# DeltaNet and MLP-mixer on one core: keys copied on chip, a copy moved behind two others, transposes moved among products, and a new order of issue

## The chip, the cores and the metric

The kernel runs on one core of a Trainium2 chip. The metric is the device time of one execution in microseconds (us). A run on one core has no sibling cores to compare with, so a run counts as slow when it is over 1.5% above the fastest run of the same kernel on the same chip, and verdicts use the other runs. The engines are TensorE (PE; its weight loads are PEld), VectorE (DVE), ScalarE (ACT), GpSimd (POOL) and the issuing engine for DMA (SP). PEclk is the share of TensorE's full clock that its throttle granted.

## The reference

```python
# B=4 batches, H=8 heads, S=768 steps, D=48; q, k, v, beta are inputs, all fp32
k_n = k / (norm(k) + 1e-6)
for t in range(S):
    y[:, :, t] = q_t @ state
    state += beta_t * outer(k_t, v_t - state^T k_t)
x = y as (B, S, H*D)                       # 4 x 768 x 384
u = x + (relu(x^T @ w_tok1) @ w_tok2)^T     # token mixer
out = u + relu(u @ w_ch1) @ w_ch2           # channel mixer
```

## The kernel before

The recurrence is done in chunks of 64 steps: 48 steps of it, 12 for each batch. Each chunk needs the inverse of a triangular matrix (groups of chunks share one inversion on VectorE, a long chain of small subtractions and additions), then a few matmuls p_q, p_w, p_s. The mixers of a batch follow when its 12 steps are done. The whole kernel is written as generators, called jobs; each `yield` ends a piece of work, and a long string says which job does its next piece. Every engine executes its own pieces in the order in which that string issued them.

One step of the recurrence (cut):

```python
            p_q = ps_seq([128, NP, 2 * D], "p_q")
            for p in range(NP):
                nc.tensor.matmul(p_q[:, p], kqt[:, 2 * p + cc], s0[:, p])
            yield
            for i in range(2):                       # VectorE, two subtractions
                nc.vector.tensor_tensor(out=r_bd[...], in0=p_q[lo, ...], in1=v_st[...], op=ALU.subtract)
            nc.scalar.copy(y, p_q[hi])               # ScalarE, the copy of y
        ...
        yield
        p_w = ps_seq([128, NP, 2 * D], "p_w")        # TensorE, needs r_bd
        ...
        yield
        for r, e in zip(PAR, ends):
            nc.scalar.copy(w_bd[r, :, e], p_w[lo, :, e])   # ScalarE, the copies of w
        yield
        p_s = ...                                    # TensorE, needs w_bd
```

In the built program the copy of y waits for the two subtractions that were issued just ahead of it.

The channel mixer (cut), and the matmuls that only keep TensorE's clock up:

```python
        for c in range(0, NCH, 2):
            u_t = ...                                # transposes p_ut of two chunks of u, copied to u_t by ScalarE
            for m in range(NM):
                p_c = ...                            # u_t times wc1; ReLU of p_c on ScalarE
            ...                                      # eight products p_o with wc2, each added to xb by VectorE

    def keep_warm(m):                                # job x: m=1 (128 columns), job z: m=4 (512 columns)
        while True:
            nc.tensor.matmul(p_warm[:, 0:m], zero, zero[:, None, :].to_broadcast([128, m, 128]))
            yield
```

## Time and profile before

| before | value |
|---|---|
| runs (us) | 750.45, 755.32, 749.22 |
| profiled run (us) | 748.09 |
| first p_c matmul, start of the dense stage (us) | 166.7 |
| last matmul (us) | 742.4 |
| TensorE gaps over 0.15 us between them, sum (us) | 23.9 |
| of these, the largest three (us) | 11.31, 3.16, 2.75 |

Up to the first p_c, VectorE and the chain through it set the pace ("the start" below). From there TensorE does ("the dense stage"), and what counts is whether it ever stands still. The lines are shown in the prediction.

### The profile page before, as it was taken

Reading aid. Unit: us, or ns where it says so; the run is one execution under the profiler, and the core shown is the slowest. Engines: PE = TensorE matmul, PEld = TensorE weight load, DVE = VectorE, ACT = ScalarE, POOL = GpSimd, SP = SyncE. Lnnn points to the kernel's source line nnn. Section 1 sums busy time; section 2 is a strip of 40 time slices with the busy share of each in tenths; the row PEclk is TensorE's granted clock in tenths of the full one; section 3 lists DMA queues with packets and bytes.
Section 4 is the critical chain, followed back from the end, with each engine's and each line's share of the span. In section 5 each row is a group of like instructions: output and inputs, shape, how many; then the busy total and the mean of one; then the engine's idle time right before and its main releaser. Section 6 shows DMA issues by size and latency. Waiting matters only on the chain. (4 is left out here: it accounts for less than half of the span.)

```text
span 746.3 us, 18528 instructions
## 1 busy us (share of the span) xinstructions
PE 700.5 (94%) x7734; PEld 598.1 (80%) x7734; DVE 438.7 (59%) x1163; ACT 237.1 (32%) x553; POOL 100.7 (13%) x118
## 2 busy tenths in 40 slices
PE   8889998899999999999899998999949999999997
PEld 5558876568789899868888987879939987998987
DVE  6987688998878934349744688334753332321312
ACT  4546375535522123323144321133112322011120
POOL 1222135214330101020111110010000000000000
PEclk9997599999999999999999999999969999999999
DMA  8843356645544033251134210211010100000000
GB/s 164 170 101 78 83 123 144 163 107 121 106 89 89 1 87 61 42 116 33 38 71 88 50 43 29 57 32 33 22 27 11 40 7 1 13 10 22 0 22 22
DMA packets 151107, 46.92 MB, mean 63 GB/s; under 512 B 142416, under 2 KB 145488, under 8 KB 151024
## 3 DMA queue, kind: packets, MB, share of 16 engines
q1 hardware_dynamic: 151024, 45.74, 28.4%
q8 instruction: 61, 1.00, 0.6%
q14 instruction: 22, 0.18, 0.1%
HBM read 36.27 MB, written 9.44 MB: 61 GB/s over the span
## 5 line engine op out<-in xcount | busy, mean ns | idle before, releaser
L813 PE MATMUL p_c<-u_t,wc 128*128 128x256 f32 x864 | 198.8, 385 | 12.7 <-ACT u_t L782 12.7
L813 PEld LDWEIGHTS p_c<-u_t,wc 128*128 128x128 f32 x864 | 162.2, 192 | 34.6 <-ACT u_t L782 13.5
L833 PE MATMUL p_o<-wc,r 128*128 128x192 f32 x720 | 127.6, 328 | 3.5 <-ACT r L820 3.5
L833 PEld LDWEIGHTS p_o<-wc,r 128*128 128x128 f32 x720 | 116.6, 190 | 5.7 <-ACT r L820 4.3
L820 ACT ACTIVATE r<-p_c 128x512 f32<-128x512 f32 x72 | 42.6, 597 | 126.8 <-PE p_c L813 117.7
L786 DVE TENSOR_TENSOR xb<-xb,p_o 128x192 f32<-128x192 f32 x84 | 29.4, 351 | 75.9 <-PE p_o L833 75.5
L525 DVE TENSOR_TENSOR x<-x,sub 128x84 f32<-128x84 f32 (+24 forms) x178 | 60.9, 342 | 6.1
L520 DVE TENSOR_TENSOR sub<-x 128x84 f32<-128x84 f32 (+24 forms) x178 | 58.1, 326 | 4.2
L806 DVE TENSOR_TENSOR s<-r 128x384 f32<-128x384 f32 x24 | 14.0, 583 | 76.9 <-ACT r L820 76.9
L833 PE MATMUL p_o<-wc,s 128*128 128x192 f32 x288 | 52.8, 333 | 3.1 <-DVE xb L786 3.1
L233 POOL TENSOR_TENSOR w_f<-w_f,d 128x384 uint32<-128x384 uint32 (+1 forms) x34 | 34.4, 1015 | 125.2 <-DVE w_f L226 65.7
L833 PEld LDWEIGHTS p_o<-wc,s 128*128 128x128 f32 x288 | 47.4, 193 | 4.1 <-DVE xb L786 3.6
L323 POOL TENSOR_TENSOR v_st<-v_st,nrm 128x384 f32<-128x384 f32 x24 | 21.2, 884 | 209.1 <-DMA v_st<-in_v_dram 137.6
L704 ACT COPY xb<-p_q 64x384 f32<-64x384 f32 x33 | 15.7, 475 | 101.5 <-DVE rw_bd L700 101.4
L382 POOL TENSOR_TENSOR mb<-mask_c,cs 128x512 f32<-128x512 f32 x20 | 22.5, 1125 | 163.3 <-DVE cs L364 157.6
L408 DVE TENSOR_TENSOR gm<-p_g,mb 128x512 f32<-128x512 f32 x48 | 31.8, 685 | 14.6 <-PE p_g L402 13.9
L729 DVE TENSOR_TENSOR s_bd<-s_bd,p_s 48x192 f32<-48x192 f32 x60 | 21.4, 357 | 32.1 <-PE p_s L721 31.2
L782 ACT COPY u_t<-p_ut 128x384 f32<-128x384 f32 x24 | 10.6, 481 | 81.7 <-PE p_ut L778 81.6
L696 PEld LDWEIGHTS p_q<-s_bd,kqt 128*128 128x128 f32 x264 | 33.0, 191 | 3.7 <-issue 1.9
L700 DVE TENSOR_TENSOR rw_bd<-p_q,v_st 64x192 f32<-64x192 f32 x66 | 23.1, 349 | 21.6 <-PE p_q L696 11.1
L166 PE MATMUL p_warm<-warm 128*128 128x128 f32 (+1 forms) x102 | 35.5, 458 | 0.0
L696 PE MATMUL p_q<-s_bd,kqt 128*128 128x96 f32 x264 | 35.0, 275 | 0.3 <-DVE s_bd L729 0.2
(110 smaller groups left out, 1002.4 us busy)
## 6 DMA issues: line engine op xcount, KB each, us to landing
d<-in_moe_w_ch_dram SPq DMA_DIRECT2D x24, 384.0 KB, 3.8
kpad<-in_k_dram SPq DMA_DIRECT2D x24, 192.0 KB, 4.1
kst<-in_k_dram SPq DMA_DIRECT2D x96, 48.0 KB, 3.1
qpad<-in_q_dram SPq DMA_DIRECT2D x24, 192.0 KB, 3.4
v_st<-in_v_dram SPq DMA_DIRECT2D x96, 48.0 KB, 2.7
out_dram<-xb SPq DMA_DIRECT2D x24, 192.0 KB, 1.9
n_dram<-gm SPq DMA_DIRECT2D x72, 32.0 KB, 1.9
gm<-w_dram SPq DMA_DIRECT2D x72, 32.0 KB, 2.2
```

The lines of the kernel that those rows point to most:

```text
L166: nc.tensor.matmul(p_warm[:, 0:m], zero, zero[:, None, :].to_broadcast([128, m, 128]))
L233: nc.gpsimd.tensor_tensor(out=f, in0=f, in1=lo, op=ALU.add)
L382: scaler.tensor_tensor(out=mb, in0=mask_c[:, None, None, :].to_broadcast([128, NP, 2, C]), in1=cs[:, :, :, None].to_broadcast([128, NP, 2, ...
L408: nc.vector.tensor_tensor(out=blocks(gm)[:, :, cc, 0 : 2 * C].rearrange("s p (two n) -> s p two n", two=2), in0=p_g[cc], in1=mb[:, :, cc, ...
L520: nc.vector.tensor_tensor(out=tmp, in0=y[:, :, 0:s, s : s + 1].to_broadcast([n, k, s, w]), in1=y[:, :, s : s + 1, s + 1 : m].to_broadcast( ...
L525: nc.vector.tensor_tensor(out=y[:, :, 0:s, s + 1 : m], in0=y[:, :, 0:s, s + 1 : m], in1=tmp, op=ALU.add,)
L696: nc.tensor.matmul(p_q[:, p], kqt[:, 2 * p + cc], s0[:, p])
L700: nc.vector.tensor_tensor(out=r_bd[r, :, ends[i ^ cc]], in0=p_q[lo, :, ends[i]], in1=v_st[r, :, cc], op=ALU.subtract,)
L786: nc.vector.tensor_tensor(out=xb[:, c, e], in0=xb[:, c, e], in1=p, op=ALU.add)
L813: nc.tensor.matmul(p_c[:, k], piece_of(wc1, cb, f * 128)[:, f * 128 : (f + 1) * 128], u_t[:, cb], start=(cb == 0), stop=(cb == NCB - 1),)
L820: nc.scalar.activation(r2[:, m], p_c, ACTF.Relu)
L833: nc.tensor.matmul(p, a[:, m], wc2[:, m, j], start=(start and m == 0), stop=(m == NM - 1), skip_group_check=True,)
```

## The change

The intent: fewer small DMA transfers in the first 40 us, a copy of y that no longer makes ScalarE wait for VectorE, transposes of u that no longer stand in a row before p_c, and an order of issue made for all that. The diff, with the order string cut:

```diff
-            if src is k:
+            if src is k and u >= RU:
                 yield from stacked(kst, k, u)
+
+        heads = kpad[u % NK].rearrange("t (p par) d -> t p par d", par=2)
+        for cc in range(2 if u < RU else 0):
+            for par in range(2):
+                nc.scalar.copy(kst[PAR[par ^ cc], :, cc], heads[PAR[cc], :, par, 0:D])
+                yield
@@ recurrence
-            nc.scalar.copy(y, p_q[hi])
@@
             nc.scalar.copy(w_bd[r, :, e], p_w[lo, :, e])
+        if c > 0:
+            nc.scalar.copy(y, p_q[hi])
         yield
@@ mixer
-        for c in range(0, NCH, 2):
+        def turn_pair(c):
             u_t = mlp_pool.tile([128, NCB, 2 * U], FP32, name="u_t", bufs=1)
             for i in range(2):
                 turn(u_t, c + i)
                 yield
+            return u_t
+
+        u_t = yield from turn_pair(0)
+        for c in range(0, NCH, 2):
@@ after the first product
             add(c, 0, p_o)
             yield
+            if c + 2 < NCH:
+                u_t = yield from turn_pair(c + 2)
@@ order
-    w1*3 y w1 w3 y b w3*3 k0*4 y k0 w1 k0 x y z y*2 w3 z p0 b y b y k1 p0 k1 p0*2 y p0*8
     ... (60 lines)
+    b y w3*3 w1 k0 y k0 x k0*2 k3 k0*2 p0*2 y p0 y b*2 p0*3 k1*2 p0 w3 p0*3 k1*2 k2 k1 x
     ... (60 lines)
```

## The prediction

> **What bounds the kernel now.** I read the page first, then the busy time of each engine in stretches of 20 us, then TensorE's own timeline for its gaps, then the timeline of all engines around the largest gaps.
>
> ```profile
> PE 700.5 (94%) x7734; PEld 598.1 (80%) x7734; DVE 438.7 (59%) x1163; ACT 237.1 (32%) x553; POOL 100.7 (13%) x118
> PE   8889998899999999999899998999949999999997
> DVE  6987688998878934349744688334753332321312
> PEclk9997599999999999999999999999969999999999
> ```
>
> Two stages have different limits. Up to about 165 us, TensorE's row is high partly because of the matmuls that only keep it warm (51 wide and 216 small ones in the program), and DVE's row is at 7 to 9: the first VectorE addition of the token mixer (L772) starts at 160.7 us with 142.4 us of VectorE work ahead of it (the durations of the 354 instructions before it, added up). Single gaps over 0.15 us on VectorE come to 21 us there, 6.5 of them before 13.2 us and 10.3 between 67 and 102 us, where it waits for the first recurrence steps. So VectorE sets the pace of the first stage. From the first p_c matmul (166.7 us) to the last (742.4 us) TensorE sets it. I added up its remaining instructions at their warm spacing (p_c 0.216 us a pass, p_o 0.163, and so on): 553.7 us of the 575.7. The rest is gaps.
>
> The timeline of TensorE around 540 us shows the largest gap (start, us, engine, line, operation, in brackets the idle time before it and what ended it):
>
> ```profile
> 539.50 0.60 PE L586 MATMUL p_z<-t,gm 32*32 32x32 f32 x27
> 551.42 18.23 PE L813 MATMUL p_c<-u_t,wc 128*128 128x256 f32 x72 [11.31 <-ACT u_t L782]
> ```
>
> The same stretch for all engines, with lines left out:
>
> ```profile
> 549.57 0.72 DVE L700 TENSOR_TENSOR rw_bd<-p_q,v_st 64x192 f32<-64x192 f32 x2
> ...
> 550.38 0.48 ACT L704 COPY xb<-p_q 64x384 f32<-64x384 f32 x1 [11.94 <-DVE rw_bd L700]
> ...
> 550.88 0.48 ACT L782 COPY u_t<-p_ut 128x384 f32<-128x384 f32 x1
> ```
>
> TensorE waits for the second copy of u_t. That copy is ready from 539 us, but it stands on ScalarE behind the copy of y (L704), which waits for the two L700 subtractions, which stand on VectorE behind some 11 us of the inversion (L520, L525). At 457 us the same copy of y holds up three ReLU evictions:
>
> ```profile
> 457.90 0.48 ACT L704 COPY xb<-p_q 64x384 f32<-64x384 f32 x1 [9.15 <-DVE rw_bd L700]
> ...
> 458.40 1.57 ACT L820 ACTIVATE r<-p_c 128x512 f32<-128x512 f32 x3
> ...
> 459.06 4.17 PE L833 MATMUL p_o<-wc,r 128*128 128x192 f32 x24 [3.16 <-ACT r L820]
> ```
>
> All TensorE gaps over 0.15 us after the first p_c: 11.31, 3.16, 2.75 (363 us, an addition of p_o that is late on VectorE), 0.68 twice (p_c waits for u_t at 682 and 713 us), 0.65 (a transpose of u, 438 us), and eleven smaller ones that sum to 4.7; together 23.9 us.
>
> **What the Trainium skill says.** "PSUM — Partial Sum Buffer", section "Engine vs sequencer instructions": "ScalarE/VectorE/GpSimdE queues are strict FIFO." The trace agrees: the copy of u_t starts 0.50 us after the copy of y that it doesn't depend on. "TensorE: Matmul & The Clock Gate", Part 1: after about 3.4 us without work the array falls back to half its clock until it has been busy again. The trace agrees: 0.66 granted in 540 to 560 us, and 72 passes of p_c took 18.23 us after the gap against 15.81 in the last pair, 2.4 us more. "DMA: Bandwidth & Descriptors", "Specifications": pieces under 512 B don't reach line rate. A row of kst is 48 floats, 192 B; 142416 of 151107 packets are under 512 B, and the DMA engines are 79 to 86% busy at 159 to 184 GB/s in the first 40 us. "SBUF — State Buffer", "Who interferes with whom": a VectorE operation with two inputs in SBUF contends with GpSimd's reads. The trace agrees: an L525 addition of 128x168 took 1.06 us beside GpSimd at 361 us and 0.33 us alone at 457 us.
>
> **The change, part by part.**
>
> *First keys on chip.* For four units 4 DMAs of 48 KB each become 4 ScalarE copies of 64x192. Removed: 16 issues, which fill about 0.65 us each of the issuing queue (2.58 to 3.16 us for each set of four), 10.9 us of a queue that runs without a break until 41 us. Added: 16 copies by some 0.31 us (the row L716, same shape), 5.0 us on ScalarE, which has 17.5 us of work in the first 33 us. The first unit gains nothing: its kpad, issued at about 2.1 us as now, lands some 4 us later (the median of the row kpad), four copies and the square take 1.8 us, so VectorE gets its first sum at about 8 us, as now (7.95). And from 13.2 us to the first inversion (33.4 us) VectorE has one gap over 0.15 us, 0.28 us; in the built program 71 VectorE instructions stand ahead of that inversion before and after, 27.5 us each. A relief of DMA can't shorten that. Gain: 0 to 1 us.
>
> *Copy of y behind those of w.* In the program the copy of y then needs no wait of its own: it comes after w, so the subtractions are long done. What stood behind it on ScalarE no longer waits for VectorE's inversion. This removes most of the 3.16 us; I take 2.5. The cost: p_s takes the PSUM buffer of p_q (two buffers in rotation p_q, p_w, p_s), so it now has to wait for the copy of y, 0.45 us later than for w. In the program TensorE has under 1.25 us of other work between p_w and p_s in 9 of the 33 steps with this copy; there p_s started 0.17 us after w so far, so each loses some 0.3 us: plus 2.5 us.
>
> *Transposes of u among the products.* 8 of 12 pairs get them after the first product instead of after the last. The 0.68 twice and some of the 0.65 go: minus 1.5 us. The second PSUM buffer comes free in time, since three transposes (0.65 us) cover the first copy (0.48 us).
>
> *New order.* In the order of before, 10.6 us of VectorE and no TensorE work stand between the last p_z and the p_c of the 11.31 us gap; in the new one no stretch of the program after the first p_c has more than 1.5 us of VectorE or ScalarE work without a matmul. The last inversion's chain, with what stands between, is 36.3 us of VectorE beside 43.1 us of TensorE work, where it was 30.3 beside 26.9. So the gap goes, and its half clock: minus 11.3 and minus 2.4. The other late chains are as uneven as before (33.1 beside 31.2, 25.0 beside 23.7, 30.8 beside 30.1 us), so I keep the 2.75 and the small gaps. TensorE work after the first p_c is 551.9 us against 553.7: minus 1.8. Ahead of the first L772 VectorE has 141.9 us against 142.4; it could lose some of its 10 us of waiting in the first steps, or gain some: minus 0.5. Eight fewer wide warm matmuls lie where TensorE isn't the bound: 0.
>
> The sum: -0.5 (keys) -2.5 + 2.5 (y) -1.5 (u) -11.3 -2.4 -1.8 -0.5 (order) = -18.0 us. 750.45 - 18.0 = 732.4 us.
>
> **Rivals.** (1) The inversion stays the limit and the wait only moves: p_w stands on TensorE's own queue and needs the same subtractions, so a late VectorE stops TensorE itself rather than ScalarE. For it: VectorE is still heavier than TensorE in three of the chains; 2.75 us of such waiting is there now. Against: the last chain, where the loss was, now has the larger TensorE side. It would give back 5 to 8 us: 738 to 741. (2) The copy of y on the path of p_s costs in all 33 steps rather than 9, up to 0.45 us each: plus 12 us more at the worst, 744. Against: in most steps p_s started 0.2 to 5 us after w, behind other matmuls. (3) The start is bound by DMA after all, through data that VectorE gets early enough only by chance, and the freed 10.9 us of the queue bring the whole first stage forward by 5 us or more: 727 or less. Against: VectorE's gapless 20 us. (4) The freed queue only makes later loads collide, and ScalarE (22.5 us of work ahead of the first inversion, 17.5 before) delays unit after unit: plus 2 to 3 us.
>
> **Range and chances.** The 13.7 us of the one gap are the safest part; the other terms are small and of both signs, and an order of some thousand steps can hide a new wait of a few us anywhere. I put eight in ten on 723 to 743. The border of 2% is at 735.4, 3 us above my number: faster 0.62, same 0.36, slower 0.02.
>
> **What would show it.** Right: no TensorE gap over 4 us after the first p_c, granted clock of 1.00 there throughout, gaps summing to 8 to 13 us; the first p_c between 162 and 168 us; copies of y with no wait for L700 in front of them; p_s waiting for ScalarE by up to 0.45 us in some steps; the first inversion still near 33 us with VectorE gapless before it. Wrong: a new gap of several us at a p_w that waits for L700, or the first p_c earlier than 160 or later than 171 us.

## The result, and the profile after

The changed kernel took 731.05 us (median of 733.07, 731.02, 731.08 and 730.3), the kernel before 749.86 us beside it. The ratio is 0.9738, with a 95% interval of 0.9688 to 0.9788: faster. A ratio here and below is the mean time of one kernel's fast runs over that of the other's of the same rounds, so it isn't quite the ratio of the medians that are quoted.

The number is within 1.4 us of the prediction, which is luck in part: the profile shows that two errors in it cancelled. Of the profiled runs (748.09 and 733.07 us, 15.0 apart where the medians are 18.8 apart):

| us | before | after | measured change | predicted |
|---|---|---|---|---|
| first p_c | 166.7 | 174.6 | +7.9 | -1.0 (keys -0.5, order -0.5) |
| first p_c to last matmul | 575.7 | 553.0 | -22.7 | -17.0 (all other terms) |
| gaps in that stretch | 23.9 | 6.3 | -17.6 | -12.8 (-11.3, -2.5, -1.5, +2.5) |

The page of the kernel after, busy time and the rows of slices:

```profile
PE 700.8 (96%) x7774; PEld 605.5 (83%) x7774; DVE 439.8 (60%) x1163; ACT 242.1 (33%) x569; POOL 99.4 (14%) x118
...
PE   8797998999999999999999999999999999999998
DVE  5998678799796792545965559723776432311212
...
PEclk9987579899899999999999999999999999999999
```

The hole in TensorE's row at 540 us is gone, and the clock is full from the twelfth slice on. But PEclk has its lowest digits, 7 and 5, in the fourth to sixth slice (55 to 110 us), at a place that the prediction left out of its sum. The kernel before has a 7 and a 5 there too.

What TensorE waited for between 176 us and the end, in the kernel after (waiter, releaser, us in total, times, longest):

```profile
PE p_o L844 <- DVE xb L793: 3.0, 4, 0.9
PE p_z L592 <- DVE t L587: 0.9, 2, 0.6
PE p_q L702 <- DVE s_bd L741: 0.7, 1, 0.7
PE p_q L702 <- DVE s_bd L736: 0.6, 1, 0.6
PE p_o L844 <- ACT u_t L789: 0.6, 2, 0.3
PE p_w L718 <- DVE rw_bd L706: 0.5, 1, 0.5
```

This is the whole answer: nothing over 0.9 us. p_c waits for nothing, and p_s is not in the list, though the prediction charged it 2.5 us.

The timeline that matters most is not where the old gap was. It is around 346 us in the kernel after (start, us, engine, line, operation, lines left out):

```profile
345.55 1.10 PE L702 MATMUL p_q<-s_bd,kqt 128*128 128x96 f32 x8 [0.61 <-DVE s_bd L736]
...
348.35 15.71 PE L824 MATMUL p_c<-u_t,wc 128*128 128x256 f32 x72
...
351.15 0.60 ACT L831 ACTIVATE r<-p_c 128x512 f32<-128x512 f32 x1 [1.82 <-PE p_c L824]
...
365.07 0.72 DVE L706 TENSOR_TENSOR rw_bd<-p_q,v_st 64x192 f32<-64x192 f32 x2
...
365.85 0.88 PE L718 MATMUL p_w<-rw_bd,gm 128*65 128x96 f32 x8
```

The two subtractions (L706) end over 19 us after their p_q, because the inversion stands ahead of them on VectorE. In the kernel before, the worst was 17.5 us and the one of the 11.31 us gap 11.6 us. So the new order doesn't bring the subtractions earlier; here it brings them later than ever. What is different is that 72 passes of p_c and six ReLUs run meanwhile, because the copy of y is not there to block ScalarE. None of the 33 copies of y has a wait over 0.15 us in front of it; in the kernel before 27 of them waited for L700. That put the prediction's attribution in doubt: it gave the 11.3 us to the order and 2.5 us to the move of y.

### The profile page after: what moved, and what is told of

Read it like the earlier page. It is cut to its first block, busy times and chain, and to the rows that moved or that the text cites.

```text
span 730.9 us, 18603 instructions
## 1 busy us (share of the span) xinstructions
PE 700.8 (96%) x7774; PEld 605.5 (83%) x7774; DVE 439.8 (60%) x1163; ACT 242.1 (33%) x569; POOL 99.4 (14%) x118
## 3 DMA queue, kind: packets, MB, share of 16 engines
q1 hardware_dynamic: 146672, 44.95, 28.7%
## 4 chain that ended last, share of the span: by engine, by line
PE 67%; DVE 22%; ACT 3%; issue 3%; DMA 2%; SPq 1%; POOL 0%; ACTq 0%; DVEq 0%; POOLq 0%
PE p_o L844 20%; PE p_c L824 16%; DVE sub L526 6%; DVE x L531 5%; PE p L762 4%; PE p_q L702 4%; PE p_s L728 3%; PE p_w L718 3%; PE p_g L408 3%; PE p_h L775 3%; PE p_z L592 2%; PE p_x L601 2%; PE p_warm L166 1%; PE p_warm L176 1%; DVE gm L414 1%
## 5 line engine op out<-in xcount | busy, mean ns | idle before, releaser
L824 PE MATMUL p_c<-u_t,wc 128*128 128x256 f32 x864 | 195.6, 381 | 0.0
L721 ACT COPY rw_bd<-p_w 64x192 f32<-64x192 f32 x72 | 22.4, 311 | 99.1 <-PE p_w L718 98.1
L844 PE MATMUL p_o<-wc,s 128*128 128x192 f32 x288 | 51.0, 329 | 2.5 <-DVE xb L793 2.5
L408 PE MATMUL p_g<-kqt 64*64 64x128 f32 x768 | 30.8, 304 | 7.3 <-ACT kqt L397 7.3
L736 DVE TENSOR_TENSOR s_bd<-s_bd,p_s 48x192 f32<-48x192 f32 x60 | 21.4, 357 | 25.9 <-PE p_s L728 25.0
L706 DVE TENSOR_TENSOR rw_bd<-p_q,v_st 64x192 f32<-64x192 f32 x66 | 23.0, 349 | 20.2 <-PE p_q L702 14.1
L728 PEld LDWEIGHTS p_s<-rw_bd,gm 128*112 128x112 f32 x288 | 32.9, 178 | 2.7 <-issue 0.3
```

The lines of the kernel that those rows point to most:

```text
L408: nc.tensor.matmul(p_g[cc][PAR[i ^ cc], p], kqt[PAR[i], 2 * p + cc, 0], kqt[PAR[i], 2 * p + cc],)
L728: nc.tensor.matmul(p_s[0 : C + D, p], gm[:, 2 * p + cc, C:], w_bd[:, p])
L824: nc.tensor.matmul(p_c[:, k], piece_of(wc1, cb, f * 128)[:, f * 128 : (f + 1) * 128], u_t[:, cb], start=(cb == 0), stop=(cb == NCB - 1),)
L844: nc.tensor.matmul(p, a[:, m], wc2[:, m, j], start=(start and m == 0), stop=(m == NM - 1), skip_group_check=True,)
```

## The experiments

Twelve kernels were run. They combine the three edits of code (K: keys on chip, Y: copy of y behind w, U: transposes of u among the products) with the order of before, that of after, or a splice: the order of before up to the first step of the token mixer, then the order of after with the pieces already done left out. Each splice and each single edit issues the same work; only the warm matmuls differ in number. "First p_c", "dense" and "gaps" are from the profiled run of each kernel, worked out as in the table above; "clock" is PEclk at 80 to 100 us.

| kernel | edits, order | first p_c | dense | gaps | clock | median (before beside it) | ratio (95%) |
|---|---|---|---|---|---|---|---|
| before | none, before | 166.7 | 575.7 | 23.9 | 0.61 | 749.86 | 1 |
| after | K Y U, after | 174.6 | 553.0 | 6.3 | 0.50 | 731.05 (749.86) | 0.9738 (0.969 to 0.979) |
| y_alone | Y, before | 163.7 | 556.9 | 8.9 | 1.00 | 727.42 (749.14) | 0.9756 (0.967 to 0.984) |
| order_alone | none, after | slow run | slow run | | | 767.40 (749.14) | 1.0208 (1.007 to 1.035) |
| undo_y | K U, after | 172.7 | 569.6 | 18.7 | 0.53 | 748.30 (749.14) | 1.0025 (0.999 to 1.006) |
| undo_keys | Y U, after | 175.7 | 550.9 | 6.2 | 0.54 | 732.27 (749.14) | 0.9806 (0.972 to 0.989) |
| parts_old_order | K Y U, before | 159.0 | 560.3 | 10.5 | 1.00 | 729.54 (748.61) | 0.9738 (0.969 to 0.978) |
| start_old | Y U, splice | 168.8 | 549.6 | 5.2 | 0.83 | 724.18 (748.61) | 0.9685 (0.964 to 0.973) |
| start_old_keys | K Y U, splice | 172.6 | 552.9 | 6.2 | 0.62 | 722.76 (748.61) | 0.9683 (0.963 to 0.974) |
| undo_u | K Y, after | 176.2 | 561.8 | 14.7 | 0.50 | 743.14 (748.61) | 0.9961 (0.993 to 0.999) |
| warm_new | K Y U, after, +16 warm | 176.0 | 552.3 | 6.5 | 1.00 | 732.67 (748.86) | 0.9818 (0.977 to 0.987) |
| warm_old | Y U, splice, +16 warm | 177.4 | 552.1 | 5.5 | 1.00 | 734.55 (748.86) | 0.9848 (0.980 to 0.989) |
| light_new | K Y U, after, +6 warm | 165.3 | 550.6 | 4.8 | 1.00 | 724.04 (751.96) | 0.9659 (0.961 to 0.970) |
| light_old | K Y U, splice, +7 warm | 173.1 | 550.3 | 5.7 | 0.99 | 730.35 (751.96) | 0.9736 (0.969 to 0.979) |

Two cautions. A dense stage that begins earlier has more of the other work left in it, so compare the sum of the two columns when the starts differ. And the kernel before itself spread from 740.0 to 755.8 us in 23 runs on one chip, so a difference of 3 us between kernels of different calls is no finding.

### y_alone: the copy of y moved, nothing else

```diff
-            nc.scalar.copy(y, p_q[hi])
@@ after the copies of w
+        if c > 0:
+            nc.scalar.copy(y, p_q[hi])
```

> The kernel before with one edit: the copy of y is issued behind those of w; keys, transposes of u and the order of issue stay as before. Theory 1 (the copy of y, waiting on ScalarE for late VectorE subtractions, was the whole cause of the 11.31 us and 3.16 us gaps, whatever the order): both gaps go, and the half clock after the first, so 11.3 + 2.4 + 3.2 = 16.9 us less, about 733 us; in this program the two copies of u_t stand ahead of w and y, and the next p_w stands behind 36 matmuls of p_c. First p_c unchanged near 167 us. Rival, as the prediction on record has it (the order, that is VectorE's 10.6 us of work without TensorE work beside it, makes the gap, and the move of y is worth 2.5 - 2.5): the gap near 540 us stays or only moves to p_w, and the time is 748 to 751 us.

It took 727.42 us, 21.7 less than the kernel before beside it; the ratio is 0.9756. That is some 6 us less than Theory 1 expected. In the profiles 18.8 us of the gain lie in the dense stage and 3.0 in the start, where first p_c was to stay near 167 us and came at 163.7. Those 3.0 aren't the move's: in the built programs the first 508 VectorE and 1880 TensorE instructions of both kernels are the same. The same stretch as in the prediction's fence, now in y_alone:

```profile
531.36 0.48 ACT L783 COPY u_t<-p_ut 128x384 f32<-128x384 f32 x1 [0.66 <-PE p_ut L779]
...
532.29 15.81 PE L814 MATMUL p_c<-u_t,wc 128*128 128x256 f32 x72
...
541.84 0.72 DVE L700 TENSOR_TENSOR rw_bd<-p_q,v_st 64x192 f32<-64x192 f32 x2
...
550.44 0.48 ACT L717 COPY xb<-p_q 64x384 f32<-64x384 f32 x1
```

The order is that of before, and the subtractions (L700) are as late as before, 11.6 us after p_q. But p_c starts right after the second copy of u_t and runs at full clock: 15.81 us instead of 18.23. The copy of y comes at 550 us and nobody misses it. The p_w that needs the late subtractions stands behind 36 matmuls of p_c, so TensorE doesn't notice either. Theory 1 holds for the dense stage, and the prediction's attribution falls: the same gap vanishes without the new order.

### order_alone and undo_y: the new order with the copy of y where it was

order_alone takes the new order string and no edit of code. undo_y is the kernel after with the edit above reversed.

> The order of issue of the kernel after, with the code of before: keys by DMA, copy of y ahead of p_w, transposes of u after the last product. Theory 1 (the new order relies on the late copy of y: the subtractions end up to 19.4 us after their p_q in it, at 346 us in the trace of after, while five ReLU evictions go ahead of y): ScalarE now holds these evictions, TensorE stops for 10 to 13 us near 350 us and runs at a lower clock after it, and the time is 743 to 749 us. Rival, the prediction on record (the order by itself takes away 11.3 + 2.4 + 1.8 us): about 734 us plus what the start loses.

> The kernel after with one edit: the copy of y is put back ahead of p_w. Theory 1: a gap of 10 to 13 us comes up near 350 us, with a lower clock after it, and smaller ones where subtractions end 3 to 6 us after p_q (240, 264, 310, 459, 551 us), so 743 to 749 us. Rival, the prediction on record (the move gains 2.5 us and costs 2.5): 729 to 734 us, no gap over 4 us.

order_alone came to 767.40 us (756.63 to 771.26). Theory 1 had expected 743 to 749; all four runs lie above that, by 8 to 22 us. Two of its four runs count as slow; the two fast ones (756.63 and 765.3) give a ratio of 1.0208, slower than the kernel before, but "unclear" by the rule of 2%. Its profile fell on a slow run, so only the times are used, and the excess has no shown cause; a sum under undo_u offers one. undo_y came to 748.30 us in 20 runs: the whole gain is gone. Its timeline at the place where the kernel after had its 19 us delay:

```profile
352.67 10.53 PE L823 MATMUL p_c<-u_t,wc 128*128 128x256 f32 x48
...
369.39 0.72 DVE L706 TENSOR_TENSOR rw_bd<-p_q,v_st 64x192 f32<-64x192 f32 x2
...
370.15 0.47 ACT L710 COPY xb<-p_q 64x384 f32<-64x384 f32 x1 [14.09 <-DVE rw_bd L706]
370.65 1.57 ACT L830 ACTIVATE r<-p_c 128x512 f32<-128x512 f32 x3
...
371.30 4.88 PE L823 MATMUL p_c<-u_t,wc 128*128 128x256 f32 x12 [8.11 <-ACT r L830]
```

ScalarE idles 14.09 us in front of the copy of y. Three ReLUs whose p_c is done stand behind it, p_c goes no further until they have run, and TensorE waits 8.11 us. This is the mechanism of the 11.31 us gap again, some 190 us earlier. The gap is smaller than the 10 to 13 us that I expected; p_c got through 48 passes first.

### undo_keys: the first keys by DMA again

```diff
-            if src is k and u >= RU:
+            if src is k:
                 yield from stacked(kst, k, u)
-        (the four ScalarE copies)
```

> The kernel after with one edit: the first four kst come by DMA again, at the same places in the order. In the trace of after the first p_c is 7.9 us later than before. Theory S1 (the copies on ScalarE and the later kpad delay the first units): the first p_c comes back to about 167 us and the time to 723 to 725 us. Rival S2 (the new order, which puts the units' work in another sequence, delays the start, not the copies): the first p_c stays at 173 to 176 us and the time at 730 to 733 us. S3 (the on-chip copies help, as their queue relief was meant to): first p_c later than 177 us, over 735 us.

732.27 us, first p_c at 175.7: S2. The on-chip copies are not what makes the new order's start late. With undo_u and undo_y beside it (176.2 and 172.7), all profiles of the new order from fast runs, without added warm matmuls, have the first p_c 6 us or more after that of before.

What the copies do is seen in how long VectorE stands without work before the first inversion begins (its start less the durations ahead of it, in us, one profile each):

| | keys by DMA | keys on chip |
|---|---|---|
| order of before | 6.2 (before), 5.5 (y_alone), 6.3 (start_old) | 8.2 (parts_old_order), 8.1 (start_old_keys) |
| order of after | 10.0 (undo_keys) | 7.0 (after), 6.5 (undo_u), 6.1 (undo_y) |

In the order of before they cost about 2 us, in the new one they save 3. Neither shows in the whole time: start_old and start_old_keys, below, have ratios of 0.9685 and 0.9683, and the intervals of undo_keys and after overlap.

### start_old, start_old_keys, parts_old_order: the old start, and the old order

The splice, as a few lines of the script that made the order strings:

```python
pre = before[: before.index("m0")]          # pieces up to the token mixer's first
order = pre + [the pieces of after that are not in pre, in the order of after]
```

> Order of before up to the first step of the token mixer (141 us in its trace), order of after for the rest; copy of y behind w and transposes of u among the products; the first keys by DMA, as the old start had them. Theory S2 (the new order's first part, not the on-chip keys, makes the first p_c 8 us later, and the dense stage's gain comes from the rest): first p_c at 163 to 168 us, dense stage of 551 to 556 us, 719 to 725 us in all, 6 to 10 us better than the whole change. Rival: the dense stage of the new order needs what its own start had done earlier, and loses there what the start wins: first p_c at 163 to 168 but a dense stage of 560 us or more, 728 us or more.

> As the run before it, but with the first keys copied on chip. If the on-chip copies are worth what the prediction says (0 to 1 us less) or what undo_keys showed (its first p_c was 1.1 us later than with them), it is 0 to 2 us faster than the run before it. Rival S1 (the copies delay ScalarE and the first units): first p_c 3 us or more later than in the run before it.

> The order of before with all three edits of code. If the move of y carries the gain, this is like y_alone (about 727 us there), less 1 to 3 us for the transposes of u (the two gaps of 0.68 and one of 0.65 us go) and for the keys: 723 to 727 us, first p_c at 163 to 168 us. Rival, the prediction on record (the order carries 15 us): 745 us or more.

start_old took 724.18 us, start_old_keys 722.76 us. The dense stage of the new order doesn't need its own start: 549.6 and 552.9 us. The first p_c of start_old, expected at 163 to 168 us, came at 168.8. That of start_old_keys came 3.8 us later still, at 172.6, which is the sign of Rival S1; but parts_old_order, with the same copies, had it at 159.0, and the times of the two splices don't differ. The splices look better than the whole change (24.4 and 25.9 us below the kernel before, where the whole change is 18.8 below), but the intervals of the ratios overlap a little. That start_old_keys is 0 to 2 us faster than start_old is neither borne out nor refuted.

parts_old_order has all the code and the old order: ratio 0.9738, the same as with the new order. Its 729.54 us missed the expected 723 to 727, and its first p_c came 4 us before the expected range. The transposes and the keys added nothing that can be told from y_alone. So the new order is worth nothing in sum: in the profiles its dense stage is shorter and its start longer.

The two profiles of this group gave the clue to the start. parts_old_order and start_old_keys issue the same VectorE and TensorE instructions in the same order in the whole start (in the two built programs the first 290 groups on each of these engines are identical, which takes in all that is compared here). Yet they reached the fifth subtraction of the early recurrence at 91.5 and 98.4 us. Stretches of 20 us (length, busy time and instructions of each engine, PEclk, DMA share, GB/s), first parts_old_order, then start_old_keys:

```profile
80.00:100.00 20.00, 17.00 (x620) 14.63 (x613) 18.92 (x52) 14.00 (x37) 9.61 (x10) 1.00 0.53 122
```

```profile
80.00:100.00 20.00, 19.26 (x427) 16.63 (x424) 13.04 (x41) 9.53 (x25) 5.58 (x6) 0.62 0.30 70
```

With a clock of 1.00, TensorE did 620 passes in that stretch and VectorE was busy 18.92 of 20 us. With 0.62 it did 427, TensorE looks busier (19.26), and VectorE idles. What is issued is the same; the clock differs, and 6.9 us are lost. That the clock is the cause is an inference here; the last four runs test it. start_old_keys had four runs at 720 to 724 us and two at 730, and the profiled one was one of the two.

### undo_u: the transposes of u behind the last product again

> The kernel after with the transposes of u back behind the last product. By the prediction they are worth 1.5 us, so 732 to 734 us on the scale where the kernel after has 731: gaps of about 0.7 us where p_c waits for u_t. Rival: in the new order other work of TensorE stands between the transposes and p_c anyway, and the time is the same within 0.3 us.

743.14 us, ratio 0.9961: neither the 1.5 us of the prediction nor nothing, but some 12 us above the kernel after. It was run at another time. What TensorE waited for after 176 us:

```profile
PE p_c L820 <- ACT u_t L789: 2.4, 3, 1.0
PE p_s L728 <- ACT rw_bd L721: 2.3, 2, 1.2
PE p_o L840 <- DVE xb L793: 1.9, 2, 1.3
PE p_z L592 <- DVE t L587: 1.8, 3, 0.9
PE p_x L601 <- DMA gm<-w_dram: 1.4, 1, 1.4
```

Only 2.4 us of it is p_c waiting for u_t. The rest is spread over waits that the kernel after doesn't have. The two pieces of the transposes move by twelve pieces within each pair of chunks, so every later word "m" of the order string now means another piece of work, and the neighbours that had been chosen for each wait no longer fit. So this run doesn't measure the price of the transposes. It shows how tightly the order and the code are fitted. In the old order the same edit, with the keys, was not to be told from zero.

17 us for the copy of y and 12 for the transposes on top of 731 make 760; the fast runs of order_alone, which lacks both and the keys, had 756.6 and 765.3. Two runs 9 us apart agree with that sum but don't prove it.

### warm_new, warm_old, light_new, light_old: is the late start the half clock?

In the profile of after, TensorE's clock at 60 to 100 us:

```profile
60.00:80.00 20.00, 18.16 (x520) 16.41 (x502) 15.40 (x40) 10.71 (x26) 4.43 (x5) 0.67 0.67 149
80.00:100.00 20.00, 20.00 (x373) 16.88 (x376) 11.54 (x40) 9.10 (x26) 5.54 (x6) 0.50 0.25 51
```

TensorE is shown busy for 20.00 of 20 us, and at half its clock. That isn't the busy of a bound engine. Two groups of the same matmul in that trace (32 passes of p_z, 32x32) make it plain:

```profile
55.22 0.69 PE L592 MATMUL p_z<-t,gm 32*32 32x32 f32 x32 [1.49 <-DVE t L587]
...
80.72 1.06 PE L592 MATMUL p_z<-t,gm 32*32 32x32 f32 x32
```

Three other profiles of the new order, those of undo_y, undo_keys and undo_u, have 0.50 to 0.54 there. So more matmuls that keep the clock up were put in. warm_new: 16 of 512 columns, which its trace shows at 55.7 to 62.6 us (5) and 73 to 98 us (11). warm_old: 16 in the splice.

```diff
-    j0*4 ... y r1*2 ... r1*3 ... w9 r2 ... r2*2 y
+    j0 z*2 j0 z*2 j0 z j0 ... y z r1*2 ... r1*2 z r1 ... w9 z r2 ... r2 z r2 y        (warm_new, cut)
```

> The kernel after with 16 more wide matmuls that only keep TensorE warm: 5 in the two gaps of 1.5 and 2.8 us near 54 and 57 us, 11 among the first steps of the recurrence (72 to 100 us), where the granted clock was 0.50 in every profile of the new order. Theory C (the new order's late start is mostly this half clock, on which VectorE waits 9 to 10 us between 72 and 102 us): the clock there is 0.9 or more, the waiting in that stretch falls to 3 us or less, the first p_c comes at 164 to 169 us instead of 172 to 177, and the time is 722 to 727 us. Rival (the waiting is the chain from VectorE to TensorE to ScalarE itself; the added matmuls stand in it): the first p_c stays at 172 us or later, 731 us or more.

> start_old (order of before up to the token mixer's first step, order of after for the rest, first keys by DMA) with 16 more wide warm matmuls between about 62 and 95 us. Theory C: the half clock, which came at 60 to 100 us in some profiles of this order (0.61 in before) and not in others (0.89 and 1.00 in parts_old_order), never comes; the first p_c at 157 to 163 us, the runs within 5 us of each other, 712 to 717 us. Rival: no faster than start_old's 724 us, spread of its runs as there (7 us).

The clock was 1.00 at 60 to 100 us in the one, 0.92 and 1.00 in the other, and nothing was won, as the rivals had it: 732.67 us with the first p_c at 176.0, and 734.55 us with 177.4. By the ratios the 16 cost the splice something (0.9848 against 0.9685). The added matmuls stood in the chain themselves: VectorE's gaps over 0.15 us between 67 and 102 us, where it waits for the first recurrence steps, still sum to 10.1 us (warm_new) and 12.9 us (warm_old). Both sides of the question moved at once, so these two runs settle nothing about what the clock is worth. They do show that wide matmuls hold it.

The next pair had only six or seven, just where the clock was seen to fall:

```diff
-    y r1*2 j1*2 i1*2 k7*2 i1 k6 r1*3 k7 ... v2 r2*2 y
+    y z r1*2 j1*2 i1*2 k7*2 i1 k6 r1*2 z r1 k7 ... v2 r2 z r2 y        (light_new; and an x later in three places)
```

In light_new's trace the three z run at 71.3, 74.0 and 76.9 us.

> The kernel after with 3 wide warm matmuls of 512 columns and 3 of 128, all among the first steps of the recurrence (72 to about 95 us), instead of the 16 of warm_new, which held the clock at 1.00 but stood themselves in the chain. Theory C: the clock stays at 0.9 or more from 72 to 100 us at a cost of 2 to 3 us of added matmuls, where it was 0.50; two runs of the same early instructions (parts_old_order and start_old_keys) reached the fifth recurrence subtraction at 91.5 and 98.4 us with the clock up and down, so 4 to 7 us less: 724 to 728 us. Rival: too few to hold the clock (0.6 or less at 80 to 100 us), 731 to 734 us.

> start_old_keys with 4 wide warm matmuls of 512 columns and 3 of 128 among the first steps of the recurrence (about 68 to 92 us). start_old_keys had four runs at 720 to 724 us and two at 730; its profiled run was one of the latter, with a clock of 0.50 from 76 to 92 us. Theory C: the slow two are those in which this half clock comes; with it kept away all runs lie within 4 us at 719 to 725 us, none at 730. Rival: the added matmuls cost more than they hold, 727 us or more.

light_new has the lowest ratio, 0.9659: 724.04 us, all six runs within 721.25 to 725.10. But the intervals of the two splices include that ratio, and its own still overlaps that of the kernel after a little (0.961 to 0.970, 0.969 to 0.979). Its stretches:

```profile
60.00:80.00 20.00, 19.57 (x538) 15.64 (x536) 15.75 (x41) 11.20 (x28) 4.44 (x5) 0.85 0.63 144
80.00:100.00 20.00, 19.37 (x548) 16.46 (x547) 17.71 (x56) 12.63 (x35) 6.79 (x7) 1.00 0.32 61
```

With three matmuls of 1.1 us each and three of 0.5 us or less, TensorE did 548 passes at 80 to 100 us where the kernel after did 373, VectorE's gaps between 67 and 102 us fell from 10.3 to 2.2 us, and the first p_c came at 165.3 us instead of 174.6. The dense stage is about the same (550.6 and 553.0 us). So the half clock costs the new order some 9 us of its start, and Theory C holds that far.

It doesn't follow that the half clock made the start of after later than that of before. The same stretches of the kernel before:

```profile
60.00:80.00 20.00, 18.46 (x477) 16.47 (x477) 15.01 (x43) 9.21 (x24) 2.92 (x3) 0.62 0.46 98
80.00:100.00 20.00, 19.21 (x422) 16.64 (x424) 12.90 (x40) 9.43 (x25) 5.58 (x6) 0.61 0.29 67
```

The half clock was there too, from 64.8 to 95.5 us (in after from 73.3 to 100.6), and VectorE's gaps between 67 and 102 us sum to 10.3 us as well. With the clock held, the old order starts earlier in its turn:

| first p_c (us) | half clock at about 78 to 95 us | full clock there |
|---|---|---|
| order of before | 166.7 (before), 172.6 (start_old_keys) | 159.0 (parts_old_order), 163.7 (y_alone) |
| order of after | 174.6 (after), 172.7 (undo_y), 175.7 (undo_keys), 176.2 (undo_u) | 165.3 (light_new) |

(start_old lies between, with 168.8 us; the other runs with warm matmuls are left out.) From column to column the means differ by 8 to 9 us, from order to order by 4 to 5 us. So the half clock seems to cost about as much in the old order, and the new one looks later with and without it. These are single profiles that scatter: before and y_alone issue the same start, and y_alone had its half clock at 46 to 63 and 125 to 142 us instead. Up to the first addition of the token mixer (160.7 us before, 168.3 after) VectorE was busy 132.1 and 134.9 us, so 2.8 of these 7.6 us are busy time and 4.8 are waits. Its gaps over 0.15 us sum to 8.4 us in the first 20 us, where it had been 6.5 (3.8 and 0.4 of that for ScalarE's ksq), and between 72 and 102 us to 10.3 against 8.1. undo_keys waits 5.1 us for ksq, so the on-chip keys don't explain that part.

light_old missed: 730.35 us, no better than the splice without warm matmuls (0.9736 against 0.9683). In its profile the clock fell just before the first of the added matmuls (68.0 us), and was 0.50 from 68 to 80 us. Three of the four wide ones took 2.07 us instead of 1.13, within the chain. It seems that the place has to be right, and that in this order it isn't the same in every run; no run tests that.

## Why the prediction was right or wrong

**The total** was right by luck: the dense stage gained 5.7 us more than predicted, and the start lost 7.9 us where 1.0 was to be won.

**Copy of y** ("I take 2.5", "plus 2.5 us"): this is the step that failed. The prediction had itself read that the second copy of u_t stood behind the copy of y, and still booked the 11.3 us under "new order". Its argument, "10.6 us of VectorE and no TensorE work stand between the last p_z and the p_c", counted only what lay ahead of p_c in the order and did not ask which of it p_c depends on. p_c depends on none of that VectorE work except through the copy of y. The runs put the move at about the whole gain: y_alone is 21.7 us below the kernel before, 18.8 of it in the dense stage, and nothing is left of the gain in undo_y. The other half of the term, the 2.5 us of p_s, never came: p_s has no wait in the list above. In the built program of the kernel after, p_s takes the PSUM buffer of p_w in all 33 steps, not that of p_q as before; it seems that the pool gives the one that comes free first. The prediction took the assignment of the kernel before as fixed.

**New order** (-11.3, -2.4, -1.8, -0.5): by itself it won nothing; the two fast runs of order_alone have a ratio of 1.0208. With the other edits it is worth 0 within the error: 0.9738 with it, 0.9738 without. Its dense stage is shorter (549.6 to 553.0 us in the profiles with Y and U and that tail, 556.9 and 560.3 in the old order), but those of the old order began earlier and so had more work left; start and dense stage together are 715.9 to 729.5 us with the tail of after and 720.6 and 719.3 in the old order. The stated check that no stretch has more than 1.5 us of VectorE work without a matmul was true and beside the point: 19 us between p_q and its subtractions did no harm.

**Transposes of u** (-1.5): not measured cleanly. In the old order nothing can be told; in the new one the order depends on them by some 12 us.

**First keys on chip** (-0.5, "VectorE gapless before the first inversion"): about right in sum, wrong in detail. In the kernel after VectorE has gaps of only 0.30 and 0.36 us between 13.2 us and the first inversion, as foretold. But that begins at 35.6 us instead of 33.4: VectorE has 28.7 us of work ahead of it where 27.5 were counted, and its first sum comes at 8.7 us, not at 8 as before. The copies save 3 us of that in the new order and cost 2 in the old one.

**The first p_c "between 162 and 168", wrong if "later than 171"**: it was 174.6, so this check failed. The step that failed is the -0.5 us for VectorE's waits and work in the start: by the trace 4.8 us of waits and 2.8 us of busy time came on top. (The prediction compares 141.9 us of work with 142.4; added up in the traces it is 143.9 against 141.6.) What in the new order does this is known only in part: 1.9 us in the first 20 us (ksq) and 2.2 between 72 and 102 us. The sum also had no term for TensorE's clock in the start, though its own view of before had digits of 7 and 5 there. "TensorE: Matmul & The Clock Gate", Part 1, says that the activity window runs freely, so the moment of a transition varies from run to run; the two profiles of the same early instructions, 6.9 us apart with clocks of 1.00 and 0.62, agree with such a variation. I did not see it because I looked at the clock only in the stage where TensorE is the bound. In the start it is not the bound, but it lies on the chain: the 32 passes of p_z above took 1.06 us instead of 0.69.

**Readings.** Two are off without consequence for the sum. "553.7 us of the 575.7. The rest is gaps": the rest would be 22.0 us, and the gaps alone are 23.9, so the 553.7 is too much. And among the "eleven smaller" gaps are one of 1.04 and one of 0.79 us.

**Rivals.** (1), the wait moving to p_w, had one sign: a single 0.5 us. (2), p_s waiting for y, didn't occur. (3) and (4), both about the start, had the right place: the start did move, and later, as (4) had it. Of its causes, the delay by ScalarE is there (ksq, 3.8 us), but with the keys by DMA too. **Gaps** were to sum to 8 to 13 us, none over 4: they sum to 6.3, the largest 0.93. The clock was to be 1.00 throughout the dense stage: it was half from 192.7 to 199.6 us.

What stays open: what in the new order makes the start later at the same clock; how much of undo_u's 12 us is the transposes' own; what makes the clock fall in the old order in some runs and not in others; and whether the splice and a well-placed warm matmul together beat light_new.

## What to carry to other kernels

When an engine waits for a late instruction of another, ask first what stands behind it in its queue and doesn't need it. Moving that one instruction behind the next true consumer was worth as much as the whole change here, and the new order without it won nothing (ratios of 1.0025 in undo_y and 1.0208 in order_alone). A "busy" TensorE at a low granted clock can cost time also in a stage that it doesn't bound: six well-placed warm matmuls won about 9 us of start in the profiles, sixteen won nothing. And before a slow stretch is called the cause of a difference, look whether the faster kernel has it too.

## What the Trainium skill lacked or had wrong

- "TensorE: Matmul & The Clock Gate", Part 1, gives an idle window of about 3.4 us as what halves the clock. In the kernel after the clock fell at 73.3 us, where the gaps over 0.25 us between 72 and 76 us were of 0.67 and 0.52 us, and stayed at 0.50 from 76 to 100 us while TensorE was shown busy (20.00 of 20 us at 80 to 100). The page's section "A second HAM failure mode: psum-queue depth-cycling" tells of frequent short idles that make the clock oscillate, so it isn't wrong on this; what it lacks is how short and how frequent. The matmuls here were mostly small (32x32 and 48 to 64 columns). Three wide matmuls of 512 columns and three of 128 among them held it at 1.00 (light_new); four and three didn't in light_old, 0.50 from 68 to 80 us. Whether the size of the matmuls is the cause was not tested.
- No page says what a lower clock in a stage costs where another engine sets the pace: 6.9 us between two runs of the same early instructions, and 9.3 us of start between light_new and the kernel after.
